# All of x transposed on TensorE, and one cumulative-sum matmul less per chunk-batch

## The chip, the core and the metric

The kernel runs on one core of a Trainium2 chip. A core has TensorE (matmul; it writes to the PSUM banks), VectorE (DVE), ScalarE (ACT), GpSimd (POOL) and SyncE (SP), which here issues all transfers. Every engine works off its own instructions in the order in which they were issued, and waits on semaphores for the others. The metric is the device time of one execution in microseconds; lower is better.

## The reference

The first part is a linear attention with a decayed state, for 4 batches, 8 heads, 768 steps and 48 channels:

```
for t in range(S):
    cur = einsum('bhd,bhe->bhde', u * k[t], v[t])
    y[t] = einsum('bhd,bhde->bhe', r[t], state + cur)
    state = w[t][..., None] * state + einsum('bhd,bhe->bhde', k[t], v[t])
```

Its output y, as x of 3072 tokens by 384, goes into a two-layer network:

```
h = x @ w_in                 # 384 -> 2048
g = s * maximum(h, 0)**2 + b
out = g @ w_out              # 2048 -> 384
```

## The kernel before

**Chunks.** Time is cut into 6 chunks of 128 steps. One chunk of one batch, with its 8 heads, is a chunk-batch, n from 0 to 23. n = 0 and 1 are the first two chunks of batch 0 and are packed together; 2, 3 and 4 are first chunks of the other batches, and from 5 on each chunk-batch needs the state of an earlier one. n = 20 to 23 are the last chunks and make no new state.

**One chunk-batch, step by step.** The names are those of the written order.

- `load n.0` to `load n.3` bring w, r, k and v (192 KB each).
- `ln` takes log w on ScalarE (L316).
- `cum` sums the logarithms over the steps by matmuls into a PSUM tile of ring A: the exclusive sum with a strict triangle (L386), minus the inclusive sum with a negated inclusive triangle (L390), and four one-column matmuls for the total decay (L395; not for n of 20 and more).
- `exp` (L410, L412) takes exponentials of both sums at once, 768 columns, and then of the total.
- `mul` on VectorE (L449) multiplies r and k by them into prd.
- The product is transposed: for n below 9 by `tr` on TensorE (L475) with a copy `tev` on ScalarE (L498), from 9 on by a crossbar transpose issued from SP (`tev`, L505).
- `mt` (L541) makes the scores, also in ring A, which has one buffer; `msk` (L552) masks them on VectorE.
- `ymm` (L595, L604) makes y; `yev` (L649) adds the u term `yd` and writes x_sb. `rkp`, `rku`, `cd`, `yd` make that term on POOL and VectorE.
- `dmm`, `sup`, `st` bring the state forward (L636, L677, L686).
- x is transposed into xT: for n below DTX = 12 by `xtr` on TensorE (L697), three 128x128 transposes into a tile of ring B, and a copy `xev` on ScalarE (L712); from 12 on by a crossbar transpose issued from SP (L515).

Ring B in PSUM has two buffers; `tr`, `ymm`, `dmm` and `xtr` take turns in it.

**The network.** Two chunk-batches make a token tile T of 256 tokens, 12 of them. For each, `g1 T.i` (i = 0 to 7, six matmuls of 256 columns, L746) makes a piece of h in one of two buffers of h_ps; `relu` (L759, ScalarE) empties it into rh; `sq` squares it into gT on VectorE (L771) or ScalarE (L769); `g2 T.i` (four matmuls of 384 columns, L790) makes the output, and `oev` (L801) and `store` bring it out. g1 of a tile needs xT of both its chunk-batches.

**The order.** All of this is issued as one list, ORDER, a text of such names; a number with a plus stands for so many warm-up matmuls on TensorE without result (L1107). `@A`, `@D` after a name puts the step on ScalarE or VectorE; without it the program's rule decides: `sq` of odd i from tile 2 on goes to ScalarE, others to VectorE; `vb`, the cast of v, goes to POOL. The list fixes each engine's order; semaphores follow from the data. The planner's costs in `add` do not move anything once the list is given.

**What is switched.** ONE decides from which n on a chunk-batch uses one cumulative-sum matmul of 384 columns instead of two. With ONE = 24 none does. Where it is used, L390 is left out, `exp` takes the first sum and the total at once (388 columns), VectorE adds log w to the first sum (`inc`), and ScalarE takes the exponential of the negated result (`exn`):

```
out=t.rearrange(...), in0=c["cum"][:, 0, 0:HD]..., in1=c["lw"][:, :, 0:D], op=ALU.add
out=c["E"][:, 1, 0:HD], in_=c["inc"], func=AF.Exp, scale=-1.0
```

Of the kernel before, what the change touches and what calls it, by code (L numbers as in the profile page):

```python
# [44 lines left out]
xtr2 relu0.1 g10.2 sq0.0 small2 sq0.1@A ci2@D dmm1 relu0.2 g10.3 load5.0 sup1 xev2 g10.4 sq0.2
relu0.3 ci3 ymm3 relu0.4 g10.5 yev3 load4.1 xtr3 relu0.5 g10.6 co0 xev3 g10.7 relu0.6 sq0.4
colsum0 load4.2 sq0.3@A g11.0 exp4 lo2 co1 g20.4 relu0.7 lo3 g20.0 l24 sq0.5 ln5 load4.3 colsum1
sq0.6 relu1.0 g20.5 sq0.7 g11.1 load6.0 g11.2 relu1.1 mul4 cum5 relu1.2 g11.3 rkp4 load5.1 exp5
g20.1 sq1.0@A co2 g11.4 relu1.3 tr4 sq1.1 relu1.4 load5.2 st3 g11.5 sq1.3@A colsum2 co3 relu1.5
load6.1 g20.2 tev4 g20.6 vb4 small rku4 colsum3 sq1.5@A mt4 cssplit load7.0 g20.7 msk4 l25 st1  # L50
csspread g20.3 load6.2 csevac sq1.2 dmm4 ln6 g11.6 mul5 load6.3 cum6 relu1.6 load5.3 rkp5 g11.7
oev0.1 exp6 load8.0 tr5 cd4 rku5 g21.4 oev0.0 ln7 load7.1 tev5 sup4 g21.5 yd4 st2 st4 ymm4 load7.2
relu1.7 mul6 cum7 g21.0 exp7 load7.3 rkp6 yev4 tr6 sq1.7@A mt5 load9.0 sq1.4 tev6 g21.1 l27 cd5
vb5 msk5 xtr4 ln8 rku6 load8.1 g21.2 xev4 dmm5 g21.6 vb6@A yd5 sup5 load8.2 sq1.6@A cum8 l26 ymm5
mul7 exp8 load9.1 dmm6 g21.3 rkp7 yev5 vb7@A g21.7 load10.1 sup6 xtr5 cd6 l28 mt6 rku7 xev5
load9.2 oev1.0 tr7 ln9 g12.0 msk6 tev7 st5 load8.3 g12.1 yd6 relu2.0 dmm7 cum9 load10.2 relu2.1
mul8 ymm6 exp9 g12.2 load10.0 rkp8 yev6 g12.3 relu2.2 sup7 mt7 load13.0 st6 relu2.3 tr8 msk7
sq2.2@A g12.4 rkp9 store0.0 tev8 g12.5 oev1.1 sq2.0@A ymm7 load11.0 sq2.1@D mt8 relu2.4 sq2.3@D
xtr6 cd7 g22.0 vb8@A load9.3 msk8 yd7 relu2.5 g12.6 ln10 load11.3 l29 g12.7 rku9 yev7 sq2.4@A
load12.0 g22.4 xev6 relu2.6 sq2.5@D dmm8 xtr7 st7 store0.1 relu2.7 g22.1 sup8 sq2.6@A cd9 rku8  # L60
g22.5 load10.3 xev7 cum10 ln11 mul9 g13.0 exp10 load11.1 g13.1 sq2.7 mul10 g22.2 load11.2 relu3.1
g22.6 tev9 l210 cd8 relu3.0 rkp10 ln12 ymm8 cum11 sq3.0@A yd9 g13.2 load13.1 exp11 yd8 g22.3 tev10
relu3.2 g13.3 rku10 oev2.0 cum12 relu3.3 load13.2 g13.4 sq3.2 vb9@A rkp11 yev8 g22.7 ln13 cd10
load12.1 sq3.1 g13.5 mul11 exp12 xtr8 dmm9 load12.2 oev2.1 g23.4 xev8 sup9 mt9 relu3.4 g23.0 st9
relu3.5 msk9 tev11 sq3.5 g13.6 st8 vb10@A g13.7 relu3.6 sq3.4 dmm10 l211 load12.3 ymm9 sq3.3 vb11
sup10 mt10 load13.3 rku11 relu3.7 yev9 g23.5 sq3.6@A msk10 xtr9 l212 store1.1 g23.1 rkp13 xev9
g23.6 sq3.7@D g14.0 yd10 load15.0 ymm10 relu4.0 mul12 dmm11 cum13 load14.0 g14.1 st10 yev10 exp13
cd11 g23.2 store1.0 rkp12 vb12@A xtr10 load14.1 mt11 relu4.1 g14.2 mul13 sq4.1 load14.2 sq4.0@A
g14.3 sup11 relu4.2 g23.3 msk11 st11 load14.3 sq4.2@A g14.4 tev12 yd11 ln14 g23.7 relu4.3 rku12
oev3.0 cum14 relu4.4 oev3.1 ymm11 load15.1 exp14 g14.5 l213 yev11 tev13 g14.6 sq4.3@D ln15 l214  # L70
relu4.5 sq4.4 cum15 rku13 xev10 load16.0 g14.7 exp15 mul14 xtr11 g24.4 relu4.6 load15.2 g24.0 l215
sq4.6@A sq4.5@D vb14 cd12 relu4.7 g24.5 load15.3 rkp14 xev11 dmm12 mt12 vb13@A g15.0 yd12 msk12
tev14 g15.1 relu5.0 g24.1 sup12 sq5.0@A sq4.7@D relu5.1 mt13 load17.0 ymm12 ln16 g15.2 yev12 dmm13
cd13 rkp15 g24.2 xev12 msk13 g15.3 yd13 store2.1 dmm14 g24.6 sup13 relu5.3 st12 store2.0 relu5.2
cum16 mul15 ymm13 sq5.1 load16.1 g24.3 exp16 rku15 sup14 g15.4 load16.2 vb15@A yev13 mt14 load18.0
rku14 relu5.4 cd15 g15.5 xev13 ln17 msk14 g24.7 sq5.3 st13 relu5.5 g15.6 load16.3 oev4.1 sq5.2@A
ymm14 cum17 tev15 dmm15 g25.4 exp17 mul16 g15.7 store3.1 l217 oev4.0 g25.5 load17.1 rkp16 ln18
cd14 sq5.5 g25.0 relu5.6 sq5.4 tev16 cum18 l216 sup15 relu5.7 yd14 g25.6 sq5.7 g16.0 st14 yev14
exp18 store3.0 g16.1 sq5.6 relu6.0 xev14 rku16 mt15 sq6.0@A g16.2 relu6.1 msk15 vb16 load17.2
g25.7 yd15 relu6.2 g16.3 st15 load19.0 ymm15 relu6.3 g25.1 load18.1 yev15 g16.4 sq6.3@D load17.3  # L80
oev5.1 g25.2 relu6.4 dmm16 xev15 sq6.2@A g16.5 sup16 sq6.1 g25.3 mul17 relu6.5 load18.2 mt16 rkp17
cd16 g26.0 ln19 tev17 msk16 g16.6 st16 g26.1 relu6.6 oev5.0 load19.1 cum19 sq6.6@A vb17 g26.4
store4.1 sq6.5 l218 yd16 sq6.4@A g26.5 load19.2 exp19 g17.0 rku17 g16.7 relu7.0 rkp18 load18.3
ymm16 relu6.7 g17.1 yev16 g17.2 store4.0 cd17 relu7.1 sq6.7@D xev16 mt17 mul18 relu7.2 dmm17 g26.2
sq7.1 sup17 load20.0 sq7.0@A g26.3 msk17 g17.3 rkp19 load20.1 g17.4 load19.3 oev6.0 yd17 ymm17
relu7.4 load20.2 g26.6 rku18 yev17 relu7.3 g26.7 tev18 sq7.2 g17.5 vb18 ln20 g27.0 sq7.4 l219
relu7.5 sq7.3@D xev17 g17.6 st17 oev6.1 sq7.5 g27.1 relu7.6 mul19 load21.0 dmm18 sq7.6@A cum20
g17.7 vb19 cd18 exp20 tev19 g27.4 rkp20 relu7.7 g27.5 sq7.7 mul20 load20.3 dmm19 g27.2 rku20 sup18
mt18 tev20 g18.0 msk18 rku19 g27.3 relu8.0 store5.1 sup19 yd18 g18.1 sq8.0@A cd19 load21.1 ymm18
cd20 relu8.1 yd19 g18.2 supn20 yev18 ln21 mt19 relu8.2 xev18 g18.3 msk19 yd20 g18.4 relu8.3  # L90
load21.2 g27.6 sq8.1@D relu8.4 store5.0 cum21 sq8.2@A ymm19 exp21 oev7.0 g18.5 load22.0 yev19
vb20@A g28.0 load23.0 sq8.3@D relu8.5 sq8.4 mt20 g18.6 sq8.5@D load22.1 msk20 g27.7 xev19 rkp21
g28.1 g28.2 load22.2 mul21 g18.7 ln22 load23.1 st19 oev7.1 ymm20 relu8.6 cum22 rku21 g28.4
load23.2 exp22 g28.5 st18 tev21 relu8.7 g28.6 ln23 sq8.7@D g19.0 sq8.6@A load21.3 g19.1 relu9.0
mul22 store6.0 cum23 relu9.1 g19.2 rkp22 yev20 exp23 tev22 g19.3 rku22 relu9.2 g28.7 relu9.3 g19.4
mul23 xev20 sq9.0@A g19.5 relu9.4 supn21 cd21 mt21 sq9.2@A store6.1 cd22 g19.6 sq9.1 load22.3
msk21 vb21 relu9.5 g28.3 rkp23 sq9.3 g19.7 oev8.0 relu9.6 tev23 yd21 ymm21 sq9.6@A g29.4 relu9.7
yev21 g29.5 sq9.5 sq9.4 mt22 xev21 g29.6 oev8.1 supn22 msk22 store8.0 g29.0 vb22@A yd22 load23.3
g29.1 sq9.7 rku23 ymm22 store7.0 g29.2 yev22 g29.3 store7.1 cd23 xev22 mt23 g110.0 msk23 g29.7
relu10.0 g110.1 supn23 vb23 g110.2 yd23 oev9.1 relu10.1 ymm23 store9.1 sq10.0 relu10.2 g110.3  # L100
sq10.1@D yev23 g110.4 relu10.3 oev9.0 xev23 g210.0 relu10.4 g210.4 sq10.4 store8.1 sq10.2 g110.5
sq10.3@D g110.6 relu10.5 g210.1 sq10.5@D relu10.6 g110.7 g210.2 relu10.7 g111.0 sq10.6@A g111.1
relu11.0 g210.5 sq11.0 relu11.1 sq10.7@D g111.2 g210.3 relu11.2 g111.3 oev10.0 g111.4 sq11.1@D
relu11.3 store10.0 store9.0 g211.0 sq11.3@D relu11.4 g111.5 sq11.4@A sq11.2@A g111.6 relu11.5
g210.6 relu11.6 g111.7 sq11.5 g210.7 relu11.7 g211.1 oev10.1 g211.2 sq11.7@D store10.1 sq11.6
g211.4 g211.8 g211.3 g211.5 oev11.0 g211.6 g211.9 store11.0 g211.7 g211.10 oev11.1 g211.11
store11.1 oev11.2 store11.2
# [46 lines left out]
def kernel(  # L158
# [199 lines left out]
    def cum(n):  # L358
# [29 lines left out]
        )  # L388
        if n < ONE:
            nc.tensor.matmul(  # L390
# [757 lines left out]
```

## Time and profile before

| what | value |
|---|---|
| median of 13 runs | 191.23 us (188.85 to 192.31) |
| profiled execution | 188.85 us |
| its span | 187.0 us |
| TensorE busy | 181.4 us |
| ScalarE busy | 134.5 us |
| VectorE busy | 129.8 us |
| GpSimd busy | 104.8 us |
| bytes moved | 35.3 MB |

The span is from the first to the last instruction of the program in the profiled execution; its time also has what lies around that. Busy time is the union of an engine's instruction records. A record of a matmul holds its passage through the array, so neighbours overlap. Idle time of an engine is put down to what ended it.

### The profile page before, as it was taken

What the parts mean: (1) busy time and instruction counts of PE and PEld (TensorE: products, weight loads), DVE (VectorE), ACT (ScalarE), POOL (GpSimd) and SP (SyncE); (2) the same over time, 40 slices, a digit from 0 to 9 for tenths busy, and PEclk for the clock granted to TensorE, in tenths of its full rate; (3) what the DMA queues carried; (4) which work ended last, traced back from release to release, by engine and by line L of the source; (5) the groups of instructions that cost most, each with busy time, mean ns of one, the idle gap of its engine ahead of it and who ended that gap; (6) DMA issues with size and microseconds to landing.
All of it is one profiled execution on the core that took longest, in us unless ns stands there. A gap on an engine that the chain in (4) does not pass through costs nothing.

```text
span 187.0 us, 5062 instructions
## 1 busy us (share of the span) xinstructions
PE 181.4 (97%) x1984; PEld 143.0 (76%) x1984; DVE 129.8 (69%) x214; ACT 134.5 (72%) x254; POOL 104.8 (56%) x138
## 2 busy tenths in 40 slices
PE   7899999999999999999999999999999999999992
PEld 5477888878689778778787787887787786788872
DVE  7458795669988957797789747298689678662241
ACT  3495699787989898959949876757585698166820
POOL 3659923238997756975849495757837664200000
PEclk9999999999999999999999999999999999999998
DMA  5998999999979899999958979959779995630212
GB/s 152 250 200 242 275 378 322 323 228 183 216 156 203 181 237 181 201 244 180 216 100 207 201 162 194 220 128 219 153 164 217 179 211 122 191 107 4 84 42 84
DMA packets 122601, 35.32 MB, mean 189 GB/s; under 512 B 117329, under 2 KB 120530, under 8 KB 122578
## 3 DMA queue, kind: packets, MB, share of 16 engines
q1 hardware_dynamic: 122578, 35.01, 82.0%
q8 instruction: 15, 0.25, 0.5%
q14 instruction: 8, 0.07, 0.1%
HBM read 25.17 MB, written 4.72 MB: 160 GB/s over the span
## 4 chain that ended last, share of the span: by engine, by line
PE 87%; DMA 6%; ACT 2%; DVE 2%; issue 1%; SPq 1%; ACTq 0%; DVEq 0%
PE o_ps L790 32%; PE h_ps L746 32%; PE warm_ps L1107 4%; PE mt_ps L541 4%; DMA pkt<-in_r_dram 3%; DMA wt<-in_w_dram 3%; PE y_ps L604 2%; PE cums L386 2%; PE cums L390 2%; PE trps L475 2%; PE y_ps L595 2%; PE d_ps L636 2%; PE xt_ps L697 1%; DVE prd L442 1%; PE cums L395 1%
## 5 line engine op out<-in xcount | busy, mean ns | idle before, releaser
L759 ACT ACTIVATE rh<-h_ps 128x512 bf16<-128x512 f32 x96 | 56.0, 596 | 26.7 <-PE h_ps L746 25.8
L746 PE MATMUL h_ps<-xT,w_in 128*128 128x256 bf16 x576 | 74.7, 273 | 0.0
L790 PE MATMUL o_ps<-w_out,gT 128*128 128x384 bf16 (+1 forms) x400 | 73.3, 320 | 0.0
L746 PEld LDWEIGHTS <-w_in 128*128 128x128 bf16 x576 | 60.9, 114 | 5.1
L790 PEld LDWEIGHTS <-gT 128*128 128x128 bf16 x400 | 36.7, 98 | 16.6
L321 POOL TENSOR_TENSOR rkp<-rkt 128x384 f32<-128x384 f32 x22 | 27.4, 1247 | 14.4 <-DMA rkt<-in_k_dram 14.4
L769 ACT ACTIVATE gT<-rh 128x512 bf16<-128x512 bf16 x52 | 32.0, 628 | 0.5
L552 DVE TENSOR_TENSOR mt_sb<-mt_ps,tri_strict 128x1024 bf16<-128x1024 f32 x22 | 26.8, 1217 | 6.0 <-PE mt_ps L541 6.0
L449 DVE TENSOR_TENSOR prd<-rkt,E 128x768 bf16<-128x768 f32 x22 | 24.9, 1132 | 4.8 <-ACT E L410 2.7
L327 POOL TENSOR_TENSOR rku<-rkp,u_bc 128x384 f32<-128x384 f32 x24 | 26.4, 1104 | 2.3 <-DVE u_bc L903 2.0
L771 DVE TENSOR_TENSOR gT<-rh 128x512 bf16<-128x512 bf16 x44 | 20.5, 485 | 7.0 <-ACT rh L759 7.0
L410 ACT ACTIVATE E<-cums 128x768 f32<-128x768 f32 x24 | 19.4, 808 | 8.0 <-issue 2.9
L801 DVE SCALAR_TENSOR_TENSOR o_sb<-o_ps,s_bc,bconst 128x384 f32<-128x384 f32 (+1 forms) x25 | 14.9, 596 | 11.6 <-PE o_ps L790 11.2
L350 POOL TENSOR_TENSOR yd<-vt,cd 128x384 bf16<-128x384 f32 x22 | 18.1, 828 | 8.5 <-DVE cd L344 6.5
L649 DVE TENSOR_TENSOR x_sb<-y_ps,yd 128x384 bf16<-128x384 f32 x24 | 13.3, 552 | 11.9 <-PE y_ps L604 9.2
L686 POOL TENSOR_TENSOR st<-stmp,l 128x384 bf16<-128x384 bf16 x16 | 15.1, 943 | 4.7 <-DVE stmp L677 4.7
L1107 PE MATMUL warm_ps<-warm_sb 128*128 128x256 bf16 x84 | 13.6, 299 | 1.1 <-DVE warm_sb L1064 1.1
L344 DVE TENSOR_REDUCE cd<-rku 128x8 f32<-128x384 f32 x24 | 12.9, 543 | 1.2 <-POOL rku L327 1.2
L316 ACT ACTIVATE logw<-wt 128x384 bf16<-128x384 f32 x22 | 11.6, 526 | 2.4 <-DMA wt<-in_w_dram 2.4
L462 POOL TENSOR_TENSOR l<-E,par 128x8 f32<-128x8 f32 x20 | 5.8, 290 | 11.0 <-ACT E L412 10.0
L878 POOL CAST vb<-vt 128x384 bf16<-128x384 f32 x11 | 5.7, 518 | 10.9 <-DMA vt<-in_v_dram 10.8
L1107 PEld LDWEIGHTS <-warm_sb 128*128 128x128 bf16 x84 | 8.2, 106 | 3.2 <-DVE warm_sb L1064 1.1
(93 smaller groups left out, 178.2 us busy)
## 6 DMA issues: line engine op xcount, KB each, us to landing
out_dram<-o_sb SPq DMA_DIRECT2D x23, 192.0 KB, 2.3
wt<-in_w_dram SPq DMA_DIRECT2D x22, 192.0 KB, 3.8
rkt<-in_r_dram SPq DMA_DIRECT2D x22, 192.0 KB, 3.8
rkt<-in_k_dram SPq DMA_DIRECT2D x22, 192.0 KB, 3.8
vt<-in_v_dram SPq DMA_DIRECT2D x22, 192.0 KB, 3.7
wi_st<-in_moe_w_in_dram SPq DMA_DIRECT2D x4, 768.0 KB, 6.4
wo_st<-in_moe_w_out_dram SPq DMA_DIRECT2D x4, 768.0 KB, 6.8
pkt<-in_w_dram SPq DMA_DIRECT2D x1, 384.0 KB, 3.4
```

What stands on the lines that cost most here:

```text
L321: nc.gpsimd.tensor_tensor(out=rkp, in0=c["r"], in1=c["k"], op=ALU.mult)
L327: nc.gpsimd.tensor_tensor(out=rku.rearrange("t h d -> t (h d)"), in0=c["rkp"].rearrange("t h d -> t (h d)"), in1=u_bc, op=ALU.mult,)
L350: nc.gpsimd.tensor_tensor(out=yd, in0=c["v"], in1=c["cd"].unsqueeze(2).to_broadcast([128, H, D]), op=ALU.mult,)
L410: nc.scalar.activation(out=E[:, :, 0:HD], in_=ps[:, :, 0:HD], func=AF.Exp)
L449: nc.vector.tensor_tensor(out=prd[:, :, :, 0:D], in0=c["rk"], in1=c["E"][:, :, 0:HD].rearrange("t x (h d) -> t x h d", h=H), op=ALU.mult,)
L552: nc.vector.tensor_tensor(out=m.rearrange("s g p t -> s (g p) t"), in0=c["mt_ps"].rearrange("s g p t -> s (g p) t"), in1=(masks[n % 2] if ...
L746: nc.tensor.matmul(ps[:, f, :], lhsT=w_in_sb[ft // FPP][:, kt, :].rearrange("p (m j) -> p j m", j=FPP)[:, ft % FPP, :], rhs=xT[T][:, kt, : ...
L759: nc.scalar.activation(out=rh, in_=hs[T, i], func=AF.Relu)
L769: nc.scalar.activation(out=g, in_=rh, func=AF.Square)
L771: nc.vector.tensor_tensor(out=g, in0=rh, in1=rh, op=ALU.mult)
L790: nc.tensor.matmul(os_[T, k][:, cols], lhsT=gT[T][:, ft, tt * 128 : (tt + 1) * 128], rhs=w_out_sb[ft // FPP][:, ft % FPP, cols], start=(ft ...
L1107: nc.tensor.matmul(warm_ps, lhsT=warm_sb[:, 0:128], rhs=warm_sb, start=True, stop=True)
```

## The change

Two constants and the list change; the functions are as they were. From n = 8 on `cum` has one 384-column matmul, and `inc` and `exn` come in 16 times. All 24 chunk-batches transpose x on TensorE and copy it on ScalarE. The list is another permutation of the steps: warm-up matmuls are 74 instead of 84; by its suffixes 62 squares go to ScalarE and 34 to VectorE (52 and 44 before), and 10 casts of v to ScalarE and 14 to POOL (13 and 11 before).

```diff
-ONE = 24
+ONE = 8
 DTK = 9
-DTX = 12
+DTX = 24
...
 ORDER = """
-load0.0 load_u load0.2 load0.1 load2.0 load0.3 ln0 +15 u_mm ln1 load3.1 +1 cum0 exp0 load3.0 +5
-cum1 l20 mul0 load2.1 exp1 rkp0 +1 tr0 load2.2 ln2 mul1 tev0 +6 cum2 load3.2 u_ev +2 tr1 exp2 rku0
-li0 tev1 l21 cd0 rkp1 load3.3 vb1@A +14 mt0 vb0@A msk0 rku1 ln3 load2.3 +5 dmm0 mul2 +5 cum3
-load4.0 exp3 sup0 +5 tr2 rkp3 st0 cd1 +1 mt1 tev2 yd0 msk1 li1 rkp2 ci0 li2 +13 ymm0 mul3 li3 mt2
-l22 yev0 yd1 tr3 msk2 +1 ymm1 lo0 tev3 vb2 rku2 yev1 +2 xtr0 +1 mt3 xev0 rku3 xtr1 cd2 ln4 +1 dmm2
-xev1 sup2 yd2 vb3@A cd3 +6 g10.0 ci1@A msk3 ymm2 l23 yd3 dmm3 g10.1 yev2 relu0.0 cum4 lo1 sup3
...
+load0.0 load0.1 load_u load0.2 load2.0 ln0 ln1 load2.1 +18 cum0 load2.2 u_mm exp0 load0.3 +2 cum1
+l20 mul0 li0 exp1 rkp1 u_ev +1 tr0 load3.1 ln2 mul1 tev0 load3.2 +6 cum2 rku1 +2 tr1 exp2 load2.3
+l21 tev1 mul2 vb0@A l22 cd1 +14 mt0 rkp2 vb1@A msk0 +5 dmm0 load3.0 rkp0 tr2 sup0 +1 mt1 tev2 li1
+rku0 st0 msk1 ci0 load3.3 rku2 cd0 +13 mt2 li2 ymm0 yd0 msk2 vb2@A yd1 +1 ymm1 li3 yev0 rkp3 ln3
+xtr0 yev1 xev0 +3 cum3 cd2 rku3 dmm2 xtr1 exp3 load4.0 sup2 +6 dmm1 xev1 mul3 lo0 ci1@A +2 ymm2
+g10.0 l23 cd3 yd2 sup1 g10.1 relu0.0 vb3 yev2 tr3 relu0.1 small2 yd3 g10.2 tev3 dmm3 ci2@D g10.3
+relu0.2 xtr2 sup3 mt3 sq0.0@A load4.1 g10.4 sq0.1 relu0.3 msk3 ci3 g10.5 relu0.4 lo1 xev2 ymm3 ln4
+sq0.2 relu0.5 g10.6 sq0.3 load4.2 yev3 cum4 relu0.6 load5.0 xtr3 g10.7 co0 xev3 lo2 g11.0 relu0.7
...
+msk7 st7 g21.3 sq2.2@A store0.0 sq2.1 rkp8 g12.6 oev1.0 sq2.3 load10.1 ymm7 relu2.6 st6 xtr6 g22.4
+yev7 ln10 load10.2 mul8 relu2.5 g22.0 ln11 xtr7 sq2.4 load12.0 g22.5 xev6 sq2.6@A load10.3 cum10
+vb9 g12.7 xev7 inc10 vb8 exp10 tr8 load11.1 sq2.5@D relu2.7 g22.1 l29 mul9 exn10 g13.0 load11.2
...
 """
```

More of the change, by code (lines that the diff above doesn't have):

```diff
@@ L44 @@
-xev1 sup2 yd2 vb3@A cd3 +6 g10.0 ci1@A msk3 ymm2 l23 yd3 dmm3 g10.1 yev2 relu0.0 cum4 lo1 sup3
[L45 to L107, printed above, removed]
+load0.0 load0.1 load_u load0.2 load2.0 ln0 ln1 load2.1 +18 cum0 load2.2 u_mm exp0 load0.3 +2 cum1
+l20 mul0 li0 exp1 rkp1 u_ev +1 tr0 load3.1 ln2 mul1 tev0 load3.2 +6 cum2 rku1 +2 tr1 exp2 load2.3
@@ new lines @@
+sq0.4 sq0.5 g20.0 relu1.0 sq0.6 sq0.7 colsum0 exp4 lo3 g11.1 g11.2 co1 relu1.1 small g20.4 mul4
+g11.3 load6.0 colsum1 rkp4 g20.1 ln5 relu1.2 tr4 rku4 relu1.3 load4.3 cum5 sq1.0@A g11.4 st1 exp5
+g11.5 co2 g20.5 tev4 load5.1 sq1.3 load5.2 colsum2 sq1.1@A st3 co3 mt4 load7.0 relu1.4 g20.6
+relu1.5 cd4 g11.6 load6.1 msk4 sq1.5@A colsum3 ln6 g20.7 yd4 sq1.4@A load6.2 cssplit g11.7 sq1.2@A
+l25 l24 vb4@A csspread load5.3 cum6 csevac g20.2 mul5 exp6 load8.0 dmm4 g20.3 rkp5 sup4 ln7
+load6.3 tr5 oev0.0 ymm4 rku5 tev5 cum7 load7.1 yev4 g21.0 oev0.1 exp7 l26 xtr4 mul6 load7.2 g21.1
@@ new lines @@
+xev4 mt5 relu1.6 cd5 vb5 load7.3 g21.4 relu1.7 st2 msk5 yd5 dmm5 g21.2 ln8 load9.0 sq1.7@A st4
+sup5 tr6 cum8 vb6 store0.1 tev6 ymm5 rkp6 g21.5 yev5 exp8 load8.1 g21.6 inc8 l27 sq1.6@A dmm6 xtr5
+mul7 g21.7 load8.3 xev5 exn8 mt6 rkp7 sup6 vb7@A load8.2 g12.0 msk6 load9.1 g12.1 rku7 ln9 tr7
+oev1.1 relu2.0 load10.0 rku6 cum9 relu2.1 cd7 dmm7 g12.2 inc9 tev7 l28 load11.0 g12.3 cd6 st5
+relu2.2 ymm6 yd6 sup7 load9.2 exp9 g12.4 relu2.3 sq2.0 mt7 yd7 yev6 exn9 load9.3 g12.5 relu2.4
+msk7 st7 g21.3 sq2.2@A store0.0 sq2.1 rkp8 g12.6 oev1.0 sq2.3 load10.1 ymm7 relu2.6 st6 xtr6 g22.4
@@ new lines @@
+yev7 ln10 load10.2 mul8 relu2.5 g22.0 ln11 xtr7 sq2.4 load12.0 g22.5 xev6 sq2.6@A load10.3 cum10
+vb9 g12.7 xev7 inc10 vb8 exp10 tr8 load11.1 sq2.5@D relu2.7 g22.1 l29 mul9 exn10 g13.0 load11.2
+tev8 rku8 cum11 g22.6 load12.1 relu3.0 dmm9 rkp9 exp11 cd8 g13.1 sq2.7 tev9 sup9 dmm8 g13.2 rku9
+relu3.1 inc11 sq3.0@A g22.2 mul10 relu3.2 load13.0 g13.3 exn11 load11.3 rkp10 sup8 mt8 relu3.3
+g13.4 msk8 ln12 tev10 vb10 g22.7 sq3.2@A st9 sq3.1 g13.5 oev2.1 relu3.4 yd8 cum12 store1.0 ymm8
+relu3.5 inc12 g22.3 l210 yev8 exp12 store1.1 g13.6 cd9 sq3.4@A mul11 sq3.3 xtr8 dmm10 mt9 load15.0
@@ new lines @@
+g23.0 yd9 msk9 vb11@A g13.7 st8 xev8 load14.0 g23.1 oev2.0 relu3.6 l212 rku10 sup10 load12.2 exn12
+ymm9 g23.4 sq3.5 load12.3 yev9 relu3.7 rkp11 mt10 cd10 xtr9 tev11 g23.2 msk10 xev9 l211 rku11 ln13
+g23.5 g14.0 sq3.6 load13.1 sq3.7@D cum13 load13.2 relu4.0 dmm11 g14.1 inc13 exp13 mul12 ymm10
+exn13 load14.1 g14.2 ln14 l213 cd11 relu4.1 yd10 g23.6 relu4.2 cum14 sq4.0 load13.3 g14.3 exp14
+yd11 sup11 g23.3 inc14 relu4.3 load16.0 st11 g14.4 sq4.1 oev3.0 st10 mt11 load14.2 yev10 relu4.4
+g14.5 msk11 rkp12 sq4.2@A xtr10 load15.1 sq4.3 g14.6 vb12 ln15 g23.7 rkp13 relu4.6 load15.2 ymm11
@@ new lines @@
+relu4.5 cum15 yev11 rku12 g24.0 xev10 tev12 oev3.1 g14.7 ln16 mul13 xtr11 exn14 g24.4 store2.1
+xev11 vb13 inc15 dmm12 tev13 sq4.5 g24.1 rku13 sup12 exp15 g15.0 cd12 relu4.7 l214 sq4.4 dmm13
+load17.1 sq4.7 cum16 mul14 g24.5 sq4.6@A g15.1 rkp15 cd13 relu5.0 store3.0 sup13 exn15 g24.6 tev14
+exp16 st12 inc16 g24.2 relu5.1 l216 g15.2 st13 load17.0 mt12 relu5.2 yd12 g15.3 msk12 sq5.2@A
+store2.0 yd13 g24.3 sq5.0@A load14.3 relu5.3 g15.4 rku15 oev4.0 ymm12 relu5.4 mt13 rkp14 yev12
+sq5.3 g24.7 load16.1 msk13 sq5.1 g15.5 load15.3 g25.0 cd15 relu5.5 load16.2 mul15 g15.6 sq5.5
@@ new lines @@
+sq5.4@A xtr12 ymm13 load18.0 exn16 mt14 yev13 xev12 g25.1 vb14 msk14 ln17 tev15 g15.7 rku14
+relu5.6 xtr13 oev4.1 dmm14 g25.2 l215 xev13 store3.1 relu5.7 cum17 vb15 load19.0 g16.0 inc17 exp17
+g25.4 sq5.7 sq5.6 store4.1 mul16 relu6.0 g16.1 sup14 dmm15 g25.3 relu6.1 sq6.0 load16.3 exn17
+sup15 g16.2 ln18 cd14 load17.2 g25.5 relu6.2 yd14 cum18 load18.1 g16.3 inc18 exp18 rkp16 load20.0
+ymm14 sq6.1 oev5.0 g16.4 relu6.3 sq6.2 l218 yev14 load18.2 mt15 exn18 yd15 g25.6 relu6.4 msk15
+rku16 sq6.4@A load18.3 g16.5 sq6.3 xtr14 g25.7 st15 relu6.5 cd16 store5.0 sq6.5 ymm15 st14 g16.6
@@ new lines @@
+ln19 yev15 store4.0 xev14 l217 g26.4 oev5.1 vb16@A mul17 load17.3 cum19 relu6.6 xtr15 g26.0 xev15
+inc19 exp19 load19.1 g16.7 mul18 load19.2 g17.0 relu6.7 tev16 g26.1 exn19 ln20 dmm16 g26.5 vb18@A
+sup16 load19.3 sq6.7 cum20 g17.1 vb17 inc20 relu7.0 tev17 g26.6 rkp18 sq6.6@A dmm17 relu7.1 g17.2
+st16 exp20 load20.1 dmm18 g26.7 sq7.0@A mul19 exn20 g26.2 tev18 relu7.2 rkp17 oev6.1 g17.3 sup17
+mt16 rku17 relu7.3 load20.2 g17.4 msk16 sq7.3 g26.3 yd16 relu7.4 load21.0 g17.5 sup18 sq7.2@A vb19
+cd17 sq7.1 ymm16 rku18 tev19 oev6.0 mt17 relu7.5 g27.0 msk17 l219 yd17 g27.4 st17 load21.1 g17.6
@@ new lines @@
+yev16 ymm17 st18 load21.2 xtr16 mt18 yev17 xev16 g27.5 sq7.5@D relu7.6 load22.0 sq7.4 xtr17 cd18
+g17.7 xev17 mul20 ln21 g27.1 relu7.7 dmm19 load20.3 yd18 msk18 g18.0 sq7.7 sq7.6@A g27.2 rkp19
+store5.1 sup19 relu8.0 g27.6 rku19 mt19 tev20 g18.1 msk19 rkp21 ymm18 relu8.1 g18.2 load23.0 sq8.0
+g27.3 store6.1 rku21 cd19 relu8.2 load22.1 cum21 ln22 g18.3 sq8.1@D exp21 ymm19 yd19 inc21 relu8.3
+g18.4 oev7.0 sq8.2@A rkp20 g27.7 load22.2 yev19 relu8.4 yev18 g18.5 sq8.3 rku20 oev7.1 load23.1
+mt20 relu8.5 load21.3 xtr18 xtr19 msk20 vb20@A g18.6 xev18 g28.0 load22.3 relu8.6 supn20 sq8.5@D
@@ new lines @@
+g18.7 sq8.4 xev19 store6.0 exn21 cum22 g19.0 relu8.7 inc22 rkp22 ln23 g28.1 load23.2 relu9.0 g28.4
+mul21 sq8.6@A store7.0 g19.1 exp22 supn21 cd20 exn22 g28.5 tev21 yd20 relu9.1 cum23 ymm20 exp23
+g19.2 yev20 g28.6 inc23 relu9.2 mul22 g19.3 sq8.7 exn23 g28.2 tev22 sq9.1 mul23 g19.4 sq9.2@A
+xtr20 relu9.3 cd21 g28.3 load23.3 sq9.0 sq9.3 g28.7 yd21 oev8.0 relu9.4 store7.1 g19.5 store8.0
+rku22 mt21 relu9.5 g19.6 vb22 msk21 sq9.5 st19 g29.4 vb21@A tev23 xev20 g19.7 oev8.1 relu9.6
+supn22 cd22 ymm21 sq9.4@A g29.5 yd22 yev21 relu9.7 mt22 sq9.6@A vb23 g29.0 sq9.7@D xtr21 rkp23
@@ new lines @@
+msk22 g29.6 xev21 g29.1 rku23 g110.0 ymm22 relu10.0 g110.1 yev22 mt23 cd23 relu10.1 g110.2 yd23
+msk23 xtr22 g29.7 relu10.2 supn23 sq10.0@A g110.3 xev22 ymm23 relu10.3 g110.4 yev23 g29.2 sq10.1@D
+relu10.4 g110.5 sq10.3 sq10.4 oev9.1 xtr23 g110.6 relu10.5 sq10.2 xev23 g210.0 sq10.5@D relu10.6
+g110.7 g111.0 relu10.7 g210.1 relu11.0 g111.1 g210.2 relu11.1 g111.2 sq11.0@A sq10.6@A g29.3
+sq10.7 g111.3 oev9.0 relu11.2 g210.3 sq11.1@D relu11.3 store9.0 store8.1 g111.4 sq11.2@A g210.4
+relu11.4 g111.5 g210.5 relu11.5 g111.6 sq11.5@D oev10.0 g210.6 relu11.6 sq11.3@D store10.0 g111.7
@@ L108 @@
+store9.1 g211.0 relu11.7 g210.7 sq11.4@A sq11.7@D sq11.6@A g211.1 oev10.1 g211.4 store10.1 g211.2
+g211.8 g211.5 g211.3 g211.6 oev11.0 g211.9 g211.7 store11.0 g211.10 oev11.1 g211.11 store11.1
+oev11.2 store11.2
 """
```

## The prediction

> **What bounds the kernel now.** I read the page's head first, for which engine is full and at what clock.
>
> ```profile
> span 187.0 us, 5062 instructions
> PE 181.4 (97%) x1984; PEld 143.0 (76%) x1984; DVE 129.8 (69%) x214; ACT 134.5 (72%) x254; POOL 104.8 (56%) x138
> PEclk9999999999999999999999999999999999999998
> DMA  5998999999979899999958979959779995630212
> PE 87%; DMA 6%; ACT 2%; DVE 2%; issue 1%; SPq 1%; ACTq 0%; DVEq 0%
> ```
>
> TensorE is busy in 97% of the span at the full clock, and the chain that ended last runs on it for 87%. The DMA row matters too: nearly full up to two thirds of the span. A busy TensorE may still hide gaps, because matmul ends are modelled, so next comes its timeline, where starts can be subtracted.
>
> ```profile
> 66.03 0.33 PE L390 MATMUL cums<-logw,ntri_incl 128*128 128x384 bf16 x1
> 66.19 0.24 PE L395 MATMUL cums<-ones,logw 128*128 128x1 bf16 x4
> ...
> 74.08 0.33 PE L697 MATMUL xt_ps<-identity,x_sb 128*128 128x128 bf16 x3
> 74.25 0.33 PE L636 MATMUL d_ps<-vb,prd 128*128 128x96 bf16 x4
> ```
>
> A 384-column matmul is recorded at 0.33 us, but the next starts 0.16 us later; three transposes are recorded at 0.33 us and occupy 0.17. These start-to-start times are what I count with. The windows say in which stretches other engines come near TensorE, and the waits who stands for whom.
>
> ```profile
> 48.00:72.00 24.00, 23.94 (x280) 19.12 (x279) 18.38 (x29) 21.73 (x45) 19.76 (x25) 1.00 0.97 198
> 96.00:120.00 24.00, 24.00 (x254) 18.46 (x252) 16.69 (x26) 17.47 (x36) 16.91 (x21) 1.00 0.83 177
> 144.00:168.00 24.00, 24.00 (x235) 18.70 (x234) 16.91 (x25) 14.81 (x28) 10.14 (x11) 1.00 0.72 160
> ...
> ACT rh L759 <- PE h_ps L746: 25.8, 30, 4.1
> PEld L697 <- DVE x_sb L649: 0.3, 1, 0.3
> ```
>
> (The columns are PE, PEld, DVE, ACT, POOL, clock, DMA share, GB/s.) ScalarE waits for TensorE 25.8 us in all, TensorE waits for almost nothing: from the first h matmul at 23.55 us to the end of its work near 183 us the stream is closed. In this execution a change is worth what it does to TensorE's sum of work, to the start before 23.55 us, and what gaps it opens.
>
> **The change part by part.**
>
> *Cumulative sum.* From chunk-batch 8 on, 16 matmuls of L390 go: 16 x 0.16 = **-2.6 us**, all on the path. In their place VectorE adds log w to the exclusive sum (`incl`, 16 times) and ScalarE does two exponentials of 388 and 384 elements instead of one of 768 and a small one. `incl` has the shape of L649 or L677 (128x384 with one operand in PSUM: 0.55 us), so VectorE gains 8.8 us. On ScalarE the 768 exponential holds the engine about 0.70 us to the next start, plus 0.05 for the small one; two near 0.42 (L316, 128x384 f32) are 0.84, so +0.1 x 16 = +1.6 us. New waits: `incl` stands in VectorE's queue for the sum, with products and masks behind it; `expn` stands in ScalarE's for `incl`, with rectifiers behind it. The product that follows is used by TensorE some 10 us after its sum (cumulative sum 10 at 65.9 us, its state matmul at 77.5), so an additional hop of 1 us is covered; with that cover gone it would cost 1 us each time.
>
> *x on TensorE.* Twelve chunk-batches (12 to 23) now do 3 transposes, 12 x 0.17 = **+2.0 us** on the path, and a copy by ScalarE (L712: 0.48 recorded), 12 x 0.48 = 5.7 us beside it. The transposes wait on TensorE for L649, and everything in TensorE's queue stands behind them. The twelve that exist cost 0.3 us of idle weight loading together; with nothing done wrong it is 0, with the same density 0.3: I take **+0.3**. They also take a third tile per chunk-batch out of the two-buffered ring B; until now that was so only below 12, at no visible cost.
>
> One page of the Trainium skill speaks against this. "TensorE: Matmul & The Clock Gate", Part 4 (PE-mode transpose), gives a bf16 128x128 transpose 390 ns in isolation and about 275 ns inside a kernel, and says that transposes don't count as activity for the clock. By that, 36 more would cost 36 x 0.275 = 9.9 us, and the change would end near 195 us. The rows here have three in 0.17 us, six times less, at a granted clock of 1.00, because neighbours are queued densely. I take the row.
>
> *What goes from the DMA queue.* Twelve crossbar transposes leave SP:
>
> ```profile
> L515 SPq DMA_TRANSPOSE xT<-x_sb x12: 1183/1206/1946, 97.0 to 165.2; - x12
> SPq L515 <- DVE o_sb L801: 5.5, 4, 2.7
> ```
>
> Each occupied SP 1.2 us, 14.5 us in all, and SP stood 12.6 us more before them (5.5 in the row, 4.5, 1.2, 1.0, 0.4), with loads and stores behind. All of it lies after 97 us, where TensorE had no gap in this execution. So its value here is **0**; it can count only in executions that do have gaps.
>
> *The order: other engines.* Counting the suffixes, ScalarE does 62 squares instead of 52 (+10 x 0.63 = 6.3 us), VectorE 34 instead of 44 (-4.9), and three casts of v move to POOL (-1.6 ScalarE, +1.6 POOL). Sums: ScalarE 134.5 + 1.6 + 5.7 + 6.3 - 1.6 = 146.5 us, 79% of a shorter span; VectorE 129.8 + 8.8 - 4.9 = 133.7; POOL 106. None passes TensorE. The hiding cover for all of it is the 25.8 us that ScalarE waits; it falls to some 14.
>
> *The order: start.* Warm-up matmuls fall from 84 to 74. They only fill waits, so the question is whether the waits shrink. Before, the sum of chunk-batch 3 sits ahead of the second score matmul and shares its single PSUM buffer: the sum starts at 15.21, its exponential ends at 16.74, the score matmul starts at 16.83. In the new order this sum comes after y of chunk-batch 1, and the score matmul needs only the first mask, done at 14.90. About 1.3 us are to be had; the ten warm-ups that are gone are 10 x 0.109 = 1.1. Other ends: 0 if v, now loaded after r and k of chunk-batch 2, comes too late for its cast at 12.80 us. I take **-1.1**.
>
> *The order: loads.* From 6 to 70 us loads come at the pace of the transfers: k of chunk-batch 5 lands at 43.15 and its transposes start at 45.1. The same bytes now serve a TensorE that runs ahead. w of chunk-batch 5 was issued ahead of r and k of 4 and landed at 33.3; now it follows them and lands two transfers of about 1 us later, near 35.3, then 0.53 us of logarithm, for a sum that would start near 35.5. w of 9 landed at 54.2, its sum would start near 54.2. This costs between 0 and 1.0 us; I take **+0.5**. The logarithm that waits on ScalarE has rectifiers behind it, so this is where the new order is thinner than the old one. Elsewhere it is wider: between two first-layer groups that share a PSUM buffer (L746) the least TensorE work grows from 0.8 to 1.0 us, and from the last first-layer group to its second layer from 2.0 to 3.4.
>
> *Sum.* 187.0 - 2.6 + 2.0 + 0.3 - 1.1 + 0.5 = 186.1 us of span. The profiled execution took 188.85 (1.85 around its span), so 187.95. It is the fastest of the 13 runs; the median is 2.38 higher. TensorE has no gaps in the profiled one, so slower runs must have gaps or a longer start. I suppose late transfers. Half of this I leave: the first 70 us keep their full queue, while behind 97 us SP is freed. 187.95 + 1.2 = **189.1 us**.
>
> **The rivals.**
>
> *Load-bound (0.34).* The first 70 us decide in the median run as well: loads cost the full 1.0, and the median keeps its 2.38. 187.0 - 2.6 + 2.3 - 1.1 + 1.0 + 1.85 + 2.38 = 190.8. For it: a DMA share of 0.97 in the window 48 to 72. Against: TensorE had not waited there.
>
> *ScalarE becomes the bound (0.20), slower.* A pair of chunk-batches with its token tile takes TensorE some 13 us. ScalarE then has 8 rectifiers, 5 squares, 2 logarithms, 4 exponentials, 2 copies of x, one cast: by start-to-start times 8 x 0.49 + 5 x 0.52 + 6 x 0.42 + 2 x 0.36 + 0.4 = 10.2 us; by recorded durations 8 x 0.6 + 5 x 0.63 + 6 x 0.52 + 2 x 0.48 + 0.5 = 12.5. If queue waits make the second figure true and a late x copy or `expn` adds 1 us per tile, it passes 13; rectifiers then release the two buffers of h_ps late and L746 waits. At 0.5 us for each of ten tiles: 189.1 + 5 = 194. It decides where ScalarE's work with waits exceeds 13 us per tile. For it: window 48 to 72 already has ScalarE at 21.7 of 24. Against: even there TensorE lost 0.06 us, and the twelve tiles that gain the copies lie where ScalarE was at 14.8 to 17.5.
>
> **How the numbers follow.** My forecast has 0.46, the rivals 0.34 and 0.20. Runs of this kernel scatter by 1.8%, so below 1% (189.3 to 193.1) nothing is told from no change. The forecast lies just past that line and its low side, with all of 2.38 gone, no cost of loads and no gap before the transposes, is 187.95 - 0.5 - 0.3 = 187.2, rounded to 187.0; load-bound with a slower transfer adds 1 to 2 us to 190.8, so the range goes from 187.0 to 192.8 and leaves out the ScalarE case. Most of the forecast's chance is faster (a small part falls short of 1%): 0.45 faster, 0.36 same, 0.19 slower.
>
> **What would show it.** Right: TensorE busy sum near 180 us, L390 with 6 instead of 22, L697 with 72 matmuls at 0.17 us per three; first L746 near 22.4 us; no DMA row for xT; ScalarE near 146 us with some 14 us of waits for h_ps. Wrong: gaps of TensorE before L746 behind L759 (ScalarE's bound), before the sums of 5, 7 or 9 (loads), or before L697 (x late); transposes at 0.1 us or more each would make it slower by the skill's rule.

## The result and the profile after

The changed kernel takes 187.06 us in the median of 11 runs (186.52 to 189.39); the kernel before, run beside it, takes 190.8 us (188.38 to 192.48, 48 runs). The ratio is 0.986 with a 95% interval of 0.983 to 0.989; it takes the means of fast runs alone, those within 1.5% of the fastest of their kernel, and so stands for 2.7 us, where the medians of all runs differ by 3.7 and the lowest runs by 1.9. The profiled executions are 187.16 us with a span of 185.3, and 188.85 with 187.0.

Head of the page of the changed kernel (its line numbers are 2 higher than before), with its chain of engines:

```profile
span 185.3 us, 5073 instructions
PE 179.7 (97%) x1994; PEld 142.1 (77%) x1994; DVE 133.0 (72%) x220; ACT 141.9 (77%) x277; POOL 104.2 (56%) x141
PE 83%; SPq 8%; DMA 5%; POOL 1%; issue 0%; DVE 0%
```

TensorE has hardly a gap, as before, and is busy for 1.7 us less; the span is 1.7 us shorter. ScalarE is busy for 7 us more and VectorE for 3 us more, and neither reaches TensorE. Groups by shape (line, engine, operation, count, busy us and mean ns, idle time before):

```profile
L761 ACT ACTIVATE rh<-h_ps 128x512 bf16<-128x512 f32 x96 | 56.4, 597 | 15.2 <-PE h_ps L748 14.0
L714 ACT COPY xT<-xt_ps 128x384 bf16<-128x384 bf16 x24 | 11.5, 478 | 6.8 <-PE xt_ps L699 6.8
L424 DVE TENSOR_TENSOR inc<-cums,logw 128x384 f32<-128x384 f32 x16 | 8.9, 554 | 4.9 <-ACT rh L761 1.6 <-ACT E L419 1.1 <-ACT E L434 0.7
L434 ACT ACTIVATE E<-inc 128x384 f32<-128x384 f32 x16 | 8.5, 528 | 0.0
L699 PE MATMUL xt_ps<-identity,x_sb 128*128 128x128 bf16 x72 | 7.8, 219 | 0.0
L392 PE MATMUL cums<-logw,ntri_incl 128*128 128x384 bf16 x6 | 1.9, 325 | 0.0
```

The inclusive-sum matmul is there 6 times instead of 22, the transposes 72 times instead of 36. ScalarE's wait for h fell from 25.8 to 14.0 us: its additional work went into time in which it had waited. The transposes have no idle time before them. TensorE's timeline, at the first network group, at its one gap behind the start, and near a transpose:

```profile
22.02 1.48 PE L748 MATMUL h_ps<-xT,w_in 128*128 128x256 bf16 x12
...
27.79 0.37 PE L606 MATMUL y_ps<-vb,mt_sb 128*128 128x48 bf16 x8 [0.39 <-DVE mt_sb L554]
...
100.57 0.33 PE L699 MATMUL xt_ps<-identity,x_sb 128*128 128x128 bf16 x3
100.74 0.33 PE L597 MATMUL y_ps<-st,RK 128*128 128x96 bf16 x4
```

Three transposes occupy 0.17 us, as in the first twelve chunk-batches, and the network begins 1.5 us earlier than the 23.55 us of before. With the gap of 0.4 us, before y of chunk-batch 3, the parts add up to the profiled pair: -2.6 + 2.0 - 1.5 + 0.4 = -1.7 us. They don't explain why the median fell by 2.0 us more. The experiments are about both.

### The profile page after: what moved, and what is told of

The parts are those of the page before. It is cut to its first block, busy times and chain, and to the rows that moved or that the text cites. A ratio compares the mean times of both kernels' runs of the same rounds, so it can differ in the third digit from the quotient of the medians.

```text
span 185.3 us, 5073 instructions
## 1 busy us (share of the span) xinstructions
PE 179.7 (97%) x1994; PEld 142.1 (77%) x1994; DVE 133.0 (72%) x220; ACT 141.9 (77%) x277; POOL 104.2 (56%) x141
## 4 chain that ended last, share of the span: by engine, by line
PE 83%; SPq 8%; DMA 5%; POOL 1%; issue 0%; DVE 0%
PE o_ps L792 34%; PE h_ps L748 33%; SPq L297 6%; DMA wi_st<-in_moe_w_in_dram 5%; PE mt_ps L543 4%; PE y_ps L606 2%; PE xt_ps L699 2%; PE cums L388 2%; PE y_ps L597 2%; PE d_ps L638 1%; PE trps L477 1%; SPq L305 1%; SPq L719 1%; POOL w_in L880 1%; PE cums L397 1%; PE cs_ps L831 1%
## 5 line engine op out<-in xcount | busy, mean ns | idle before, releaser
L748 PE MATMUL h_ps<-xT,w_in 128*128 128x256 bf16 x576 | 77.6, 273 | 0.1
L792 PE MATMUL o_ps<-w_out,gT 128*128 128x384 bf16 (+1 forms) x400 | 75.3, 320 | 0.0
L771 ACT ACTIVATE gT<-rh 128x512 bf16<-128x512 bf16 x62 | 37.2, 628 | 0.3
L323 POOL TENSOR_TENSOR rkp<-rkt 128x384 f32<-128x384 f32 x22 | 23.2, 1055 | 6.4 <-DMA rkt<-in_k_dram 6.3
L773 DVE TENSOR_TENSOR gT<-rh 128x512 bf16<-128x512 bf16 x34 | 16.2, 494 | 4.9 <-ACT rh L761 4.9
L714 ACT COPY xT<-xt_ps 128x384 bf16<-128x384 bf16 x24 | 11.5, 478 | 6.8 <-PE xt_ps L699 6.8
L688 POOL TENSOR_TENSOR st<-stmp,l 128x384 bf16<-128x384 bf16 x16 | 13.1, 827 | 0.4 <-DVE stmp L679 0.4
L1109 PE MATMUL warm_ps<-warm_sb 128*128 128x256 bf16 x74 | 11.6, 299 | 1.1 <-DVE warm_sb L1066 1.1
L424 DVE TENSOR_TENSOR inc<-cums,logw 128x384 f32<-128x384 f32 x16 | 8.9, 554 | 4.9 <-ACT rh L761 1.6
L880 POOL CAST vb<-vt 128x384 bf16<-128x384 f32 x14 | 8.6, 616 | 6.2 <-DMA vt<-in_v_dram 6.0
```

Source lines behind the costliest of these rows:

```text
L323: nc.gpsimd.tensor_tensor(out=rkp, in0=c["r"], in1=c["k"], op=ALU.mult)
L748: nc.tensor.matmul(ps[:, f, :], lhsT=w_in_sb[ft // FPP][:, kt, :].rearrange("p (m j) -> p j m", j=FPP)[:, ft % FPP, :], rhs=xT[T][:, kt, : ...
L771: nc.scalar.activation(out=g, in_=rh, func=AF.Square)
L773: nc.vector.tensor_tensor(out=g, in0=rh, in1=rh, op=ALU.mult)
L792: nc.tensor.matmul(os_[T, k][:, cols], lhsT=gT[T][:, ft, tt * 128 : (tt + 1) * 128], rhs=w_out_sb[ft // FPP][:, ft % FPP, cols], start=(ft ...
```

## Experiments

The theory: the time is TensorE's sum plus the start, so each switch is worth its matmuls; what the median gains beyond is scatter that went with SP's crossbar transposes. Rivals: the list alone brings it, or the scatter comes from the start.

**One sum, undone in the new list.** The list loses the words `inc` and `exn`, nothing moves.

```diff
-ONE = 8
+ONE = 24
-... cum10 vb9 g12.7 xev7 inc10 vb8 exp10 ... exn10 ...
+... cum10 vb9 g12.7 xev7 vb8 exp10 ...
```

> The changed kernel with two cumulative-sum matmuls for every chunk-batch again (ONE = 24, the inc and exn steps taken out of the list, nothing moved). Theory, TensorE's sum decides: 16 x 0.16 = 2.6 us more work on a closed stream, 187.1 + 2.6 = 189.7 in the median and in the profile. Rival, the one-matmul form costs elsewhere what it saves (VectorE's addition, a second exponential): less than 1 us slower than the changed kernel, near 187.5.

Measured: 189.8 us (12 runs, 189.05 to 190.77), ratio to before 0.9975 (0.994 to 1.0005). The sum was 16 x 0.16 = 2.6 us; the medians give 2.7 (against 187.06), the two ratios 2.2, the spans of the profiles 2.3 (187.6 and 185.3). The one-sum form is worth its matmuls in this list, or most of them; the rival's 187.5 is far off.

**Crossbar back for x, in the new list**, and **the list with neither switch**.

```diff
-DTX = 24
+DTX = 12
-... xtr12 ... xtr23 ...
```

> The changed kernel with the crossbar transpose of x from chunk-batch 12 on (DTX = 12, the xtr steps of 12 to 23 taken out, xev of 12 to 23 issued from SP at their places in the list). TensorE's sum: 36 transposes less, -2.0 us, 185.1. Rival, SP's queue and the full transfers make the median: x comes late through SP, or loads and stores behind it do, the lowest run falls below 186 but the median stays at 187 or above and the runs scatter by 3 us or more as before the change. Second rival: xT comes too late for g1 at these places, since TensorE has only 3 us of work between y and the tile that needs it, against 2.7 us of landing plus 1.2 of issue: 1 us lost for each of six tiles, 191.

> The changed kernel's list with neither switch (ONE = 24, DTX = 12): the order alone. TensorE's sum: 187.1 + 2.6 - 2.0 = 187.7, still 3 us below the kernel before in the median, because 1.5 us come from the earlier start and the rest from wider margins in the list. Rival, the switches bring what lies beyond the start (SP's freed queue): 190.8 - 1.5 = 189.3 or more, with runs that scatter by 3 us or more.

Measured: 197.38 us (6 runs, ratio 1.038, 1.033 to 1.043) and 198.71 us (6 runs, ratio 1.040, 1.033 to 1.047). The first is 10 us slower than the changed kernel with 2 us less to do on TensorE. TensorE's waits for xT in the first run and in the second:

```profile
PE h_ps L746 <- DMA xT<-x_sb: 7.4, 3, 3.2
...
PE h_ps L744 <- DMA xT<-x_sb: 8.2, 5, 2.1
```

SP's queue and TensorE at the first of these waits, and a window behind it (columns PE, PEld, DVE, ACT, POOL, granted clock, DMA share, GB/s), all of the first run:

```profile
102.03 1.33 SPq L515 DMA_TRANSPOSE xT<-x_sb  x1
103.46 1.25 SPq L505 DMA_TRANSPOSE RK<-prd  x1
104.80 1.21 SPq L515 DMA_TRANSPOSE xT<-x_sb  x1
...
107.28 0.82 PE L746 MATMUL h_ps<-xT,w_in 128*128 128x256 bf16 x6 [3.21 <-DMA xT<-x_sb]
...
108.00:112.00 4.00, 4.00 (x22) 2.53 (x21) 1.44 (x3) 2.02 (x4) 0.10 (x1) 0.57 0.89 196
```

Network groups stand for xT, in the first run 7.4 us in three waits, and both rivals of the expectation have a part in it, though their 187 and 191 us were far too low. The second was right that the room is short: in the new list 2.6 to 4.7 us of TensorE work lie between y and the tile that needs it, in the old one 4.1 to 8.0. The first was right that x comes late through SP: in the first wait the last x was written at 101.87 us, stood 2.9 us in SP's queue behind the transpose of a product, and landed at 107.15. In the other two waits it stood 1.6 and 1.9 us; for the three tiles that didn't wait, the last x was issued within 0.1 us. From the start of its issue to landing it takes 2.4 us in the median; the 1.2 us of issue are part of this, which the expectation counted twice.

A wait can be paid a second time. Behind those of 3.2 and 2.4 us, and behind the one of 2.1 us in the second run, the granted clock falls to half for 3.4 us (in the first run from 108.2 to 111.6, and again from 138.9); behind those of 1.1 to 1.9 us it doesn't. At half the rate 3.4 us do the work of 1.7, so the two falls cost up to 3.4 us (an estimate). With the waits of 7.4 and 2.0 of work less that is 8.8 of the 9.7 us by which the span is longer. So these two runs don't price the order by itself: as it stands, this order needs x on TensorE.

**One sum in the old list**, first with `inc` behind `exp`, then ahead of it.

```diff
-ONE = 24
+ONE = 8
-... cum18 ... exp18 ... mul18
+... cum18 ... exp18 inc18 ... exn18 ... mul18     (first trial)
+... cum18 ... inc18 exp18 ... exn18 ... mul18     (second trial)
```

> The kernel before with one cumulative-sum matmul from chunk-batch 8 on: inc put right behind exp, exn two network groups later, nothing else moved. TensorE's sum: -2.6 us, 188.2 in the median against 190.8. Rival, gaps of the old list decide in the median run, and TensorE's saved work becomes waiting: less than 1 us gained, 190 or more.

> The kernel before with one cumulative-sum matmul from chunk-batch 8 on, the addition inc put ahead of exp (both read one PSUM tile, and in the earlier trial VectorE stood 10.6 us for the exponential in front). If that wait with squares behind it was the loss, VectorE's waits for L417 go and TensorE's -2.6 us show: 188.2 to 189. If the old list has no room for any additional step on VectorE and ScalarE: 192 or more again.

Measured: 195.76 us (6 runs, ratio 1.024, 1.016 to 1.031) and 194.75 us (6 runs, 1.019, 1.012 to 1.026). Both miss: 2.6 us less work, and some 4 us slower. Waits of the first trial, then of the second:

```profile
DVE inc L422 <- ACT E L417: 10.6, 11, 2.3
PE o_ps L790 <- DVE o_sb L801: 2.8, 3, 1.1
```

```profile
ACT E L417 <- DVE inc L422: 9.2, 15, 1.8
PE h_ps L746 <- ACT rh L759: 1.1, 4, 0.4
```

The exponential and the addition both read the sum's PSUM tile, and in all 16 pairs of each run the second begins only when the first has ended. In the first trial VectorE stands, and TensorE misses output buffers that VectorE empties; in the second ScalarE stands, and TensorE misses h buffers. In the list that was made for one matmul and one exponential the saved matmul returns as short gaps, before L746, L790, L697 and L386. Part of the loss is not of the edit: both profiles also have a late start. From the first group of tile 2 to the end, where nearly all of the edit lies, they are 3.9 and 1.8 us longer than the first profile of before (136.3 and 134.2 us against 132.4), instead of some 2.4 shorter.

**`inc` behind `exp` in the new list.** In ten of sixteen chunk-batches the new list has it ahead.

```diff
-... inc12 ... exp12 ... exn12
+... exp12 inc12 ... exn12
```

> The changed kernel with inc put right behind exp in the ten chunk-batches that have it ahead. Both read one PSUM tile one after the other, so here VectorE waits for ScalarE with products, masks and squares behind it. If VectorE's queue has room in the changed list: within 0.5 us of 187.1. If the place of inc is what makes the one-sum form affordable: 2 us or more slower, as in the trial in the old list.

Measured: 189.23 us (12 runs, 188.06 to 190.79), ratio 0.992 (0.987 to 0.996). The profile's waits:

```profile
DVE inc L423 <- ACT E L418: 10.1, 10, 2.2
```

VectorE stands 10 us as in the old list, but here that costs 1 to 2 us: 2.2 by medians, 1.1 by the two ratios, 1.0 by the spans of the profiles (186.3 and 185.3). So VectorE has more room in this list; that the place of `inc` counts by itself is likely, but the intervals of the two ratios still touch.

**x on TensorE in the old list.** Each `xtr` stands at least 2 us of TensorE work behind its y, and `xev` behind it.

```diff
-DTX = 12
+DTX = 24
-... yev12 ... xev12
+... yev12 ... xtr12 ... xev12
```

> The kernel before with x of all chunk-batches transposed on TensorE (DTX = 24), nothing else: each xtr put at least 2 us of TensorE work behind its y and each xev at least 3 us of it ahead of the tile that needs it. TensorE's sum: +2.0 us, a lowest run near 190.4. If the crossbar in SP's queue makes the scatter, the runs lie within 2 us of one another and the median is near 191, about equal to the kernel before; if the scatter is the list's own, the median is 192.8 and the runs span 4 us.

Measured: 193.89 us (6 runs, 192.23 to 197.95), ratio 1.0145 (1.008 to 1.021), which is 1.5 to 4.0 us: in line with the 2.0 of work, and nothing gained in return. No transpose waits:

```profile
L696 PE MATMUL xt_ps<-identity,x_sb 128*128 128x128 bf16 x72 | 8.0, 220 | 0.1
```

The spread of the runs decides little, since five of the six lie within 2.2 us. The median does: it is not at 191, as it would be if the crossbar in SP's queue made the scatter. Nor is the late start gone with it: the first network group of this profile begins at 25.6 us, 2.0 later than in the first profile of before, while that kernel's crossbar transposes of x begin only at 97 us. From the first group of tile 2 to the end it takes 134.9 us instead of 132.4, 2.5 more for the 2.0 of work. So the crossbar in SP's queue is not what makes the scatter, and this part of the theory falls.

**The start.** Old start with the new list behind it (both switches on), and new start with the old list (both off).

```diff
 # words up to the first g10.0 from one list, all words not yet done from the other
-NEW[:g10.0] + NEW[g10.0:]
+OLD[:g10.0] + [w for w in NEW if w not done]      (first; dmm1 ci1 ymm2 drawn ahead)
+NEW[:g10.0] + [w for w in OLD if w not done]      (second; cd3 drawn ahead, then yd2 sup1 yev2)
```

> The changed kernel with the list of before up to the first network group and the changed list from there on (both switches on). If the earlier first group (22.0 instead of 23.5 us) carries through to the end: 187.1 + 1.5 = 188.6. If loads bound the stretch to 70 us anyway, the start is worth nothing: 187.1 to 187.5.

> The list of the changed kernel up to the first network group and the list of before from there on, with both switches off (ONE = 24, DTX = 12). If the start is worth its 1.5 us and no more: about 190.8 - 1.5 = 189.3 in the median, with a scatter of 3 us or more. If the scatter of the kernel before comes out of its start: 188 or less in the median with runs within 2 us. If the old rest has no room for an earlier start because loads bound it to 70 us: 190.5 or more.

Measured: 190.65 us (12 runs, 188.7 to 191.64), ratio 0.9974 (0.994 to 1.001); and 193.29 us (4 runs), ratio 1.015 (1.008 to 1.022). The old start takes most of the gain away: 3.6 us by medians and 2.2 by the two ratios, where 1.5 was expected. TensorE in the first run:

```profile
24.34 1.48 PE L747 MATMUL h_ps<-xT,w_in 128*128 128x256 bf16 x12
26.92 0.82 PE L747 MATMUL h_ps<-xT,w_in 128*128 128x256 bf16 x6 [1.10 <-ACT rh L760]
```

Of the profile's 3.3 us, 2.3 are in the first network group (24.34 instead of 22.02 us). TensorE then stands 1.4 us more before L747 for the rectifier, 1.1 of it behind a cast of weights on ScalarE that waits for its load. Neither profile of before stands for the rectifier there, so part of the loss may be the hybrid's own. The second hybrid is no clean test at all: at its seam TensorE is idle for 4.0 us between 20 and 30 us, and the clock falls to half from 26.7 to 33.5. It doesn't tell what the new start alone is worth.

**Both kernels once more**, unaltered.

> The changed kernel unaltered, as an anchor on the same chip as the runs beside it: 187.1 again, with most runs between 186.5 and 188.

> The kernel before unaltered, profiled once more. If its usual run near 191 is the fast one plus gaps on TensorE, a profile near 191 shows 2 us of gaps that the first profile lacks, by place; a start that is later by 2 us would speak for late first loads, gaps before L746 or L790 in the stretch from 30 to 70 us for late weights or loads. A profile near 188.9 again leaves this open.

Measured: the changed kernel 187.62 us (4 runs, 186.94 to 187.96), ratio 0.987 (0.981 to 0.992). The kernel before, against its own other runs of the day, came to 191.87 us (9 runs) and a ratio of 1.0075 (1.003 to 1.012): two sets of runs of one program differ by 0.7%, which bounds what the ratios here can tell. Its profile was taken at 192.44 us, 3.6 us longer than the first profile. TensorE's timeline of the first profile of before:

```profile
4.37 1.08 PE L899 MATMUL u_ps<-u_row,one_row 1*128 1x384 f32 x2
5.82 0.33 PE L371 MATMUL cums<-logw,hi_neg 128*128 128x384 bf16 x1
5.99 0.33 PE L371 MATMUL cums<-logw,hs_neg 128*128 128x384 bf16 x1
...
7.56 0.32 PE L371 MATMUL cums<-logw,hi_pos 128*128 128x384 bf16 x1 [0.31 <-ACT E L412]
7.72 0.32 PE L371 MATMUL cums<-logw,hs_pos 128*128 128x384 bf16 x1
...
23.55 0.82 PE L746 MATMUL h_ps<-xT,w_in 128*128 128x256 bf16 x6
```

The same view of the second profile of the same program:

```profile
4.36 1.64 PE L899 MATMUL u_ps<-u_row,one_row 1*128 1x384 f32 x2
6.77 0.53 PE L371 MATMUL cums<-logw,hi_neg 128*128 128x384 bf16 x1
7.09 0.53 PE L371 MATMUL cums<-logw,hs_neg 128*128 128x384 bf16 x1
...
8.89 0.53 PE L371 MATMUL cums<-logw,hi_pos 128*128 128x384 bf16 x1
9.21 0.53 PE L371 MATMUL cums<-logw,hs_pos 128*128 128x384 bf16 x1
...
25.44 0.82 PE L746 MATMUL h_ps<-xT,w_in 128*128 128x256 bf16 x6
```

From one 384-column matmul to the next it is 0.17 us above and 0.32 below: TensorE still runs at half its clock until about 10 us. The transfers are not late (w, k and r of the first pair land at 4.2, 6.3 and 7.4 us, against 4.1, 6.4 and 7.6). The first network group is 1.9 us later, the first of tile 2 is 3.9 later (58.5 against 54.6), and from there the distance stays: 3.6 us at the end. Between these two profiles nothing of the difference arises behind 60 us. The second 2 us lie between 25 and 58 us and are only in part seen: from 20 to 60 us TensorE is idle for 1.4 us instead of 0.2, for a network group behind a cast of weights on VectorE (0.7 us) and for products (L475, 0.5 us).

The trace's clock records say when the full clock came. In the seven profiles with the new start it was 3.8, 4.4, 5.8, 6.1, 6.2, 6.8 and 6.9 us. In the six with the old start it was 4.8, 4.8, 9.1, 10.0, 10.4 and 12.2. (The page's clock row doesn't show this: its first slices are 9 for the second profile of before too.) The first network group goes with the clock. With the new start it begins at 22.0 us in the profile with the earliest clock and at 22.6 in the two with the latest. With the old start it begins at 23.5 and 24.3 us in the two profiles with an early clock (the second has 0.65 us of other work ahead of it) and at 25.0 to 25.6 in the four with a late one. So the late clock goes with 1 to 2 us of the old start. The scatter goes with the start as well: from the lowest run to the median, of 4 to 48 runs each, it is 0.5 to 1.2 us for five of the six kernels with the new start (2.5 for the list alone), and 1.5 to 2.7 us for the five with the old one.

The two starts differ at this place. The old list has 15 warm-ups, then the u matmul (one row, fp32, 1.1 to 1.6 us), then the first sum. The new one has 18 warm-ups, then the sum, and u behind it:

```profile
1.05 3.48 PE L1109 MATMUL warm_ps<-warm_sb 128*128 128x256 bf16 x18 [1.05 <-DVE warm_sb L1066]
4.83 0.71 PE L373 MATMUL cums<-logw,hs_pos 128*128 128x384 bf16 x2 [0.30 <-DVE hs_pos L1093]
...
6.08 0.91 PE L901 MATMUL u_ps<-u_row,one_row 1*128 1x384 f32 x2
```

The Trainium skill, "TensorE: Matmul & The Clock Gate", Part 1, has a gate that opens after one busy window of about 3.4 us, on windows that run freely and not from the kernel's start. The later half-clock stretches of these runs agree with that length: 3.4 us each in the list-only and the crossbar run, 6.8 at the hybrid's seam. On that reading 15 warm-ups (3.4 us) fill a window only when it happens to begin with them; if the u matmul, on one row of the array, then doesn't count as busy, the next window fails too and a later one has to open the gate. That the u matmul is the cause is argued, not shown: the old list with only that matmul moved behind the first sum wasn't run.

## Why the prediction was right, and where not

- **Range and direction:** 189.1 was forecast, 187.06 measured, inside 187.0 to 192.8 by 0.06 us, which is luck: the change was forecast at 2.1 us and measured at 3.7 by medians. The sum for the profiled span held better: 186.1 forecast, 185.3 measured.
- **Cumulative sum, -2.6:** right, 2.2 to 2.7 when undone alone.
- **The new wait on `incl`, costed at nothing:** right in this list only. The prediction had each engine wait for the sum or for `incl`; it missed that `exp` and `incl` wait for one another. In the profile ScalarE stands 3.2 us and VectorE 1.1 for that; in the old list, where each engine stood some 10 us, the saving became a loss.
- **x on TensorE, +2.0 and +0.3:** 0.17 us per three is measured again; the +0.3 was 0. The skill's 275 ns per transpose doesn't hold in this dense stream, where one takes a fifth of that. Put into the forecast's own sum its 9.9 us would have made 197, not 195. Whether transposes count for the clock these runs can't tell: it stayed full, but they are only 7.8 of TensorE's 179.7 us. Neither the forecast nor the rivals saw that this part shortens the way from y to xT, which the new order uses.
- **Start, -1.1:** mis-sized; -1.5 in the profiled pair (22.02 against 23.55 us).
- **Loads, +0.5:** no gap before the sums of 5, 7 or 9. The one gap of this stretch, 0.4 us in the first profile and 0.8 in the second, is before y of chunk-batch 3, for its mask. ScalarE's bound didn't come either: its records grew by 11.9 us as summed (12.0), but neighbouring ones overlap, and it is busy for 141.9 us and not 146.
- **Half of the 2.38 us between profile and median would stay, the freed SP takes the other:** this step failed. Almost nothing stayed: the median lies 0.1 us below the profiled execution and 0.5 above the lowest run. And SP was the wrong place. With x on TensorE in the old list the late start was still there, and the longer execution of the kernel before loses its time before 60 us, beginning with a clock that comes 5 us later. The forecast took TensorE's full clock from a page row that reads 9 in its first slices whether the clock comes at 4.8 or at 10.0 us, and from one execution, the fastest of 13; it never asked how sure that clock was.

Median and profile together: 1.7 us of the profiled pair are shown by parts. Beyond them the medians have 2.0 us and the means of the ratio 1.0, from scatter that the new start has less of. For this, the place (the start, and up to tile 2) and its going with a late clock are shown; the cause within the start is open, and so is part of the loss between the first network group and tile 2.
